# A fused attention, channel-mix and mixture-of-attention kernel, with the order of every engine's instructions listed by hand

## The chip, the cores and the metric

One core of one Trainium2 chip. The number is device time in microseconds (us), the median of several runs of one program. A profiled execution, run apart, gives the trace. Engines: PE is TensorE's matmul, PEld its weight load, DVE is VectorE, ACT ScalarE, POOL GpSimd, SP the engine that issues most of the transfers.

## What is computed

Inputs are q, k, v of shape 4 x 8 x 576 x 64 (batch, heads, positions, width) and the weights of two further layers. The reference, cut to what matters:

```python
# 1: attention; heads 0-3 look back 32 positions, heads 4-7 at every 4th of the last 128
attn = softmax(where(mask, q @ k.T / 8, -1e9)) @ v          # -> x: 4 x 576 x 512
# 2: channel mix
x_prev = x shifted down by one position
xk, xr = mu_k * x + (1 - mu_k) * x_prev, mu_r * x + (1 - mu_r) * x_prev
k = maximum(xk @ w_k, 0)                                    # 512 -> 1024
x = sigmoid(xr @ w_r) * ((k * k) @ w_v)                     # 1024 -> 512
# 3: four experts, each a causal attention of width 64; two are kept per position
for e in range(4):
    ye = softmax(causal((x @ wq[e]) @ (x @ wk[e]).T / 8)) @ (x @ wv[e]) @ wo[e]
    out += gate(x)[e] * ye
```

## The kernel before

All is done on one core, batch by batch, in three stages that overlap. Large products (line 539) work on pairs of tiles: each operand is split into a high and a low part, and a tile of 128 x 288 results is the sum over 4 or 8 slices of three matmuls (high by high, high by low, low by high), so 12 or 24 matmuls that go into one PSUM bank.

Stage 1, batch 0, lasts some 46 us: `turn_qk` turns q and k (line 248), `attn_weights` makes scores (line 302), exponentials (lines 342, 350) and normalised weights (line 354), `attn_values` turns the weights (line 382), copies them out of PSUM (`pts`, line 383, ACT) and multiplies them with v (line 394); ACT copies each half of 288 positions into `x` (line 409). The bank for these halves ("av") is a single one, so the second half's products wait for that copy. As features of x become ready, `mix_feature` mixes them (lines 513, 514, 516, 517).

Stage 2, `dbatch`, has receptance tiles z (`receptance`, tanh on ACT, line 562), key tiles h (`keys`: relu on ACT, line 568; squaring on ACT, line 570, or DVE, line 575; the high part kh on ACT, lines 571 and 576; the low part kl on DVE, lines 572 and 578), and value tiles v (`values_of`: one DVE pass, line 584, empties the bank). In batch 0 the two halves c = 0, 1 of the 576 positions go in turn, and the weights arrive as raw 64-bit words in slices of one megabyte, which `split_cols` turns into high and low parts by five passes (lines 679, 681, 682, 687, 688) of about 0.7 to 1.2 us on ACT and DVE. The banks of the long products are "mm", three that go round; batch 0 adds others. The attention of batches 1 to 3 runs between the products of the batch before: turned on DVE (lines 271, 276), 36 score matmuls per pair of heads (line 318), nine row minima on DVE (line 337), nine exponentials on ACT (line 342).

Stage 3 makes queries, keys and values of the experts (lines 539, 888), scores (lines 982, 984, two banks "sc" in turn), row minima on DVE (line 988), exponentials on ACT (line 994), turned weights (line 1046, copied at lines 1051 and 1053), values (lines 1092, 1106) and the output products (line 1178).

The code traces instructions in program order. The framework then puts them into each engine's queue, in an order that its own model of the times chooses; each engine takes its queue strictly in turn, and semaphores hold an instruction until what it needs is done. A few places are already tied by hand:

```python
def product(o, wts, xs, kts, wsl):                       # line 532 on
    for kt in kts:
        for w, x in ((wh, xh), (wh, xl), (wl, xh)):
            marks["product"] = nc.tensor.matmul(o, w[:, kt, wsl], x[:, kt, :], start=(n == 0), stop=(n == last)).ins

def keys(dp, b, c, fo, kh, kl, xk, wts):                 # batch 0, fo below 2 or above 5
    p = ps(bank(b), f"h_{b}_{c}_{fo}")[:, :CH]
    product(p, wts["k"], xk, range(KT), slice(128 * fo, 128 * fo + 128))
    r = dp.tile([128, CH], F32, tag="r", name=f"r_{b}_{c}_{fo}", bufs=2)
    nc.scalar.activation(r, p, AF.Relu)
    nc.vector.scalar_tensor_tensor(out=r, in0=r, scalar=0.5, in1=p if b else r, op0=ALU.mult, op1=ALU.mult)
    nc.scalar.copy(kh[:, fo, :], r)
    half.tensor_sub(kl[:, fo, :], r, kh[:, fo, :].bitcast(F32))
```

A few places are already tied by hand (`tc.issue_after`, for instance so that the attention matmuls of the later batches stay behind the last long product traced).

Of the kernel before, what the change touches and what calls it, by code (L numbers as in the profile page):

```python
# [15 lines left out]

NEG = -8.0e9
BIG = 3.0e38


@with_exitstack
def tile_dilated_attention__rwkv_channel_mix__moe_attention(
# [258 lines left out]
    def attn_weights(ap, b, hp, qT, kT):  # L281
# [43 lines left out]
        for t0, t1 in ((0, 5), (5, 9)):  # L325
# [7 lines left out]
            for t in range(t0, t1):  # L333
                k0, mask = win(dil, t)
                c0 = WK * (t - t0)
                if b:
                    nc.vector.tensor_tensor_reduce(  # L337
                        out=pe[:, t, :], in0=sc[:, c0 : c0 + WK], in1=mask, scale=-0.125, scalar=BIG,
                        op0=ALU.add, op1=ALU.min, accum_out=st[:, 0, t : t + 1],
# [286 lines left out]
    def run(gen, n=None):  # L626

        while n is None or n > 0:
            try:
                next(gen)  # L630
            except StopIteration:
                return False
            if n is not None:
                n -= 1
        return True
# [133 lines left out]
    with s2:  # L769
# [190 lines left out]
        def scores(b, e):  # L960
# [8 lines left out]
            for t in ([4, 3, 2, (3, 5), 1, 0, (0, 3)] if (b, e) == (B - 1, E - 1) else [*range(NB), (0, NB)]):  # L969
# [8 lines left out]
                for i, (c0, c1) in enumerate(parts):  # L978
# [10 lines left out]
                        out=pe[:tn, PO[t] + c0 : PO[t] + c1], in0=sc, in1=m, scale=-0.125,  # L989
                        scalar=(BIG if i == 0 else st[:tn, 1, t : t + 1]),  # L990
                        op0=ALU.add, op1=ALU.min, accum_out=least,
# [253 lines left out]
        for g in gens.values():  # L1245
            assert not run(g, 1)


# [1 line left out]
_INS = ['q', 'k', 'v', 'moe_mu_k', 'moe_mu_r', 'moe_w_k', 'moe_w_v', 'moe_w_r',  # L1250
# [27 lines left out]
```

## Time and profile before

| | us |
|---|---|
| three runs | 547.4, 548.07, 548.78 |
| median | 548.07 |
| the profiled execution | 548.24 |
| its span, first to last instruction | 546.5 |
| PE busy in the span | 524.7 (96%) |
| DVE, ACT busy | 348.9 (64%), 331.2 (61%) |

A row of a timeline has the start, the length, the engine, the line and the tiles (out<-in); a bracket tells how long the engine was idle before it and what ended that. Matmuls overlap: each lasts some 300 ns by the trace but the next begins some 131 ns later in a dense stretch, so a busy PE may still issue at less than its best. The granted clock is a share of TensorE's full 2.4 GHz; 0.50 is its lower level, 1.2 GHz.

### The profile page before, as it was taken

What the parts mean: (1) busy time and instruction counts of PE and PEld (TensorE: products, weight loads), DVE (VectorE), ACT (ScalarE), POOL (GpSimd) and SP (SyncE); (2) the same over time, 40 slices, a digit from 0 to 9 for tenths busy, and PEclk for the clock granted to TensorE, in tenths of its full rate; (3) what the DMA queues carried; (4) which work ended last, traced back from release to release, by engine and by line L of the source; (5) the groups of instructions that cost most, each with busy time, mean ns of one, the idle gap of its engine ahead of it and who ended that gap; (6) DMA issues with size and microseconds to landing.
All of it is one profiled execution on the core that took longest, in us unless ns stands there. A gap on an engine that the chain in (4) does not pass through costs nothing.

```text
span 546.5 us, 12497 instructions
## 1 busy us (share of the span) xinstructions
PE 524.7 (96%) x4618; PEld 473.8 (87%) x4622; DVE 348.9 (64%) x1136; ACT 331.2 (61%) x945; POOL 96.8 (18%) x169
## 2 busy tenths in 40 slices
PE   8988987999999999999999999999998999999996
PEld 4667987889999999999999999999976988988763
DVE  4787989695667588276461526448676658665742
ACT  3679978675884484564443525237557757656852
POOL 8400000010342021221032203000213212211300
PEclk9996999899999999999999999999999999999999
DMA  9969276876455663130100420054604425516103
GB/s 164 240 215 280 78 196 145 143 136 141 96 115 137 142 141 73 49 99 34 34 1 1 93 64 1 1 131 116 146 22 110 141 69 122 131 48 168 67 33 96
DMA packets 130172, 57.64 MB, mean 105 GB/s; under 512 B 109928, under 2 KB 117184, under 8 KB 130112
## 3 DMA queue, kind: packets, MB, share of 16 engines
q1 hardware_dynamic: 129392, 55.88, 43.5%
q8 instruction: 36, 0.59, 0.5%
q0 software_dynamic: 416, 0.44, 0.4%
q10 hardware_dynamic: 304, 0.53, 0.3%
q14 instruction: 24, 0.20, 0.1%
HBM read 34.42 MB, written 10.03 MB: 81 GB/s over the span
## 4 chain that ended last, share of the span: by engine, by line
PE 73%; DVE 10%; ACT 6%; DMA 4%; SPq 4%; issue 2%; POOL 1%; DVEq 0%; ACTq 0%; POOLq 0%
PE v L539 18%; PE h L539 11%; PE z L539 5%; PE av L1092 5%; PE pv L888 5%; PE pq L539 4%; PE pk L539 4%; PE po L1178 4%; PE pt L1046 4%; PE av L394 3%; PE sc L982 2%; PE sc L984 2%; DMA rqk<-in_k_dram 2%; SPq L189 2%; PE sc L318 2%
## 5 line engine op out<-in xcount | busy, mean ns | idle before, releaser
L539 PE MATMUL v<-kh,wv_hi 128*128 128x288 f32 x256 | 75.7, 303 | 2.5 <-ACT r L568 2.0
L539 PE MATMUL h<-xh,wk_hi 128*128 128x288 f32 x256 | 76.6, 301 | 1.5 <-ACT r L568 0.9
L539 PE MATMUL h<-xl,wk_hi 128*128 128x288 f32 x256 | 75.6, 296 | 0.8 <-DVE xl L517 0.8
L539 PE MATMUL h<-xh,wk_lo 128*128 128x288 f32 x256 | 75.3, 294 | 0.4 <-DVE wk_lo L688 0.4
L539 PE MATMUL v<-kl,wv_hi 128*128 128x288 f32 x256 | 75.4, 299 | 0.0
L539 PE MATMUL v<-kh,wv_lo 128*128 128x288 f32 x256 | 75.3, 299 | 0.0
L1012 POOL TENSOR_SCALAR first<-pe,st 128x64 f32<-128x64 f32 x70 | 31.7, 495 | 151.8 <-DVE st L1006 53.4
L529 POOL TENSOR_TENSOR xl<-m,xh 128x576 fp32r<-128x576 f32 x24 | 35.2, 1484 | 129.6 <-ACT xh L528 97.1
L994 ACT ACTIVATE pe<-pe,st 128x64 f32<-128x64 f32 (+4 forms) x80 | 44.7, 561 | 19.7 <-DVE st L988 19.4
L514 DVE SCALAR_TENSOR_TENSOR m<-x,mus,m 128x288 f32<-128x288 f32 x64 | 30.4, 511 | 34.7 <-ACT m L513 34.7
L539 PEld LDWEIGHTS v<-kh,wv_hi 128*128 128x128 f32 x256 | 48.3, 190 | 3.6 <-ACT r L568 2.4
L539 PEld LDWEIGHTS h<-xh,wk_hi 128*128 128x128 f32 x256 | 47.9, 187 | 3.2 <-ACT r L568 1.4
L539 PEld LDWEIGHTS h<-xl,wk_hi 128*128 128x128 f32 x256 | 48.1, 188 | 1.1 <-DVE xl L517 1.1
L539 PEld LDWEIGHTS h<-xh,wk_lo 128*128 128x128 f32 x256 | 48.2, 188 | 0.7 <-DVE wk_lo L688 0.7
L539 PEld LDWEIGHTS v<-kh,wv_lo 128*128 128x128 f32 x256 | 48.4, 191 | 0.4
L539 PEld LDWEIGHTS v<-kl,wv_hi 128*128 128x128 f32 x256 | 48.4, 191 | 0.4
L342 ACT ACTIVATE pe<-pe,st 128x96 f32<-128x96 f32 x108 | 39.0, 363 | 13.1 <-DVE st L337 13.1
L568 ACT ACTIVATE r<-h 128x288 f32<-128x288 f32 x64 | 25.6, 406 | 34.1 <-PE h L539 27.6
L988 DVE CUSTOM_DVE_ANT_0 pe<-sc,cmask 128x64 f32<-128x64 f32 (+4 forms) x80 | 33.3, 426 | 17.6 <-PE sc L984 15.0
L578 DVE TENSOR_TENSOR kl<-r,kh 128x288 fp32r<-128x288 f32 x50 | 31.0, 625 | 16.5 <-ACT kh L576 16.2
L539 PE MATMUL z<-xl,wr_hi 128*128 128x288 f32 x128 | 38.5, 301 | 0.1
L539 PE MATMUL z<-xh,wr_hi 128*128 128x288 f32 x128 | 38.2, 304 | 0.0
(201 smaller groups left out, 1419.2 us busy)
## 6 DMA issues: line engine op xcount, KB each, us to landing
kk<-kh SPq DMA_DIRECT2D x32, 144.0 KB, 2.7
kl<-kl SPq DMA_DIRECT2D x32, 144.0 KB, 2.8
raw_in_moe_w_k_dram<-in_moe_w_k_dram SPq DMA_DIRECT2D x4, 1024.0 KB, 6.2
raw_in_moe_w_v_dram<-in_moe_w_v_dram SPq DMA_DIRECT2D x4, 1024.0 KB, 6.2
out_dram<-ob SPq DMA_DIRECT2D x14, 256.0 KB, 2.5
rqk<-in_q_dram SPq DMA_DIRECT2D x48, 72.0 KB, 2.5
rqk<-in_k_dram SPq DMA_DIRECT2D x48, 72.0 KB, 2.9
moved<-turned SPq DMA_DIRECT2D x8, 432.0 KB, 3.0
```

The source lines that it names most:

```text
L342: nc.scalar.activation(pe[:, t, :], pe[:, t, :] if b else sc[:, c0 : c0 + WK], AF.Exp, bias=st[:, 0, t : t + 1], scale=-1.0, accum_out=st[ ...
L514: nc.vector.scalar_tensor_tensor(out=m, in0=x, scalar=mus[:, 0, w, f : f + 1], in1=m, op0=ALU.mult, op1=ALU.add)
L529: nc.gpsimd.tensor_sub(lo[:, f], m[:, f], hi[:, f].bitcast(F32))
L539: marks["product"] = nc.tensor.matmul(o, w[:, kt, wsl], x[:, kt, :], start=(n == 0), stop=(n == last)).ins
L568: nc.scalar.activation(r, p, AF.Relu)
L578: half.tensor_sub(kl[:, fo, :], r, kh[:, fo, :].bitcast(F32))
L888: nc.tensor.matmul(p, x[:, kt, t0 : t0 + tn], w[:, kt, 512:772], start=(n == 0), stop=(n == 3 * KT - 1))
L988: nc.vector.tensor_tensor_reduce(out=pe[:tn, PO[t] + c0 : PO[t] + c1], in0=sc, in1=m, scale=-0.125, scalar=(BIG if i == 0 else st[:tn, 1, ...
L994: nc.scalar.activation(pb, pb, AF.Exp, bias=st[:tn, 0, t : t + 1], scale=-1.0, accum_out=st[:tn, 2, t : t + 1])
L1012: nc.gpsimd.tensor_scalar_mul(first["keys"][:, t, e % 2, :], pe[:, PO[t] : PO[t] + 64], st[:, 3, t : t + 1])
L1046: marks[f"turn {b}{e}"] = nc.tensor.transpose(pt[:kn, c0 : c0 + 128], src, ident).ins
L1092: ins = nc.tensor.matmul(av1[p0 : p0 + 64, q0 - 64 : q1 - 64], vh[kb][:kn], w[:kn, c0 : c0 + q1 - q0], start=(kb == blocks[0]), stop=(kb = ...
```

## The change

A table gives, for ACT ("Activation"), SP, DVE, POOL and PE, the order of issue by numbers: n is the n-th instruction of that engine in program order. `issue_in_order`, called at the end of the kernel function, ties each listed instruction behind the one listed before it on its engine, with an edge that carries no semaphore. Left out of the lists are four of the 40 filler matmuls of stage 1 (line 76), one DVE subtraction (line 836) and the first two POOL instructions.

Numbers that matter: ACT 48, 50, 71 are copies into x (line 409), 49, 67, 70, 72 copies of turned weights (line 383), 66 an exponential (line 350), 68 and 142 weight passes (line 679), 69 and 52 weight casts (line 687), 83 the tanh of a z tile, 56 and 77 casts of mixed features, 154 and 155 relu and cast of the last key tile of half 0, 157, 149-151, 159, 153, 152, 156 exponentials. DVE 140 and 153 are squarings, 136, 141, 142, 154 make kl, 143 and 144 are transposes, 155-156, 145-149 and 157-158 row minima, 138 is a weight pass, 106, 108, 110, 112 mix features. PE 209-212 and 217-222 are an attention half, 261-263, 271-273, 563-565 and 584-586 transposes, 655-678 the first value tile, 717-740 and 770-793 the next two, 533-550 and 616-633 scores of the next batch, 979-990, 991-1002, 1021-1032 and 1033-1044 the first four z tiles of batch 1.

```diff
+ORDER = {
+    "Activation": (
...
+        "61-65 31 47 34 49 48 66 35 67-68 50-51 70 72 69 71 52-53 73-74 54 75 55 76 83 56 77-78 88 92 90 94 79 96 84 "
+        "93 86 82 87 89 95 91 80 106 108 102 104 81 97-98 110 114 103 101 107 105 100 99 109 85 111 115 112 116-119 "
+        "123 120 124 121 125-126 113 122 127-129 133 130 134 131 136 135 137-138 132 139 144 140-141 145-148 154 "
+        "161-162 155 157 149-151 159 153 152 156 142 163 158 143 177 160 164 170-171 173-174 179-180 168 175 172 169 "
...
+    "DVE": (
...
+        "52-53 65 49 66 50 67 51 68 20 54-55 40 21 56 69 57-58 41 73 70 74 71-72 42 75 43 76-80 59 81 60-61 82 62 83 "
...
+        "94 115 105 120 116 121-122 117 123-125 128 127 118 129 126 130-132 134-135 133 140 136 143-144 141-142 153 "
+        "155-156 145-147 154 157-158 148-149 137 165 150 184 151 166 138 159 152 160 177 161 139 167-171 178-180 "
...
+    "PE": (
...
+        "249 260 140-143 239-248 252-256 202 257-259 270 282 214-215 148-153 203-204 216 195-200 205-208 261-263 "
+        "271-272 209-212 217-222 273 283-285 264-269 274-281 286-291 293-294 305-306 329-332 341-345 307-310 333-335 "
...
+        "472-487 497-502 488-496 503-505 509-520 506-508 521-529 551-556 530-532 557-562 572-583 634-645 655-663 "
+        "533-550 664-676 717-722 677-678 723-731 770-775 732 616-633 776-778 563 584-585 564-565 779-781 586 782-787 "
...
+        "979-984 951-954 971-978 991-996 985 1021-1027 986-990 1028-1032 997-1000 1033-1035 1001-1002 1036-1044 "
...
+def issue_in_order(tc):
+
+    traced = [i for i in tc.nc.cur_bb.bb.instructions
+              if i.opcode not in ("RegisterMove", "BassTileRelease", "TileRelease", "TilePoolBoundary")]
+    for engine, runs in ORDER.items():
+        mine = [i for i in traced if str(i.engine) == "EngineType." + engine]
+        behind = None
+        for run in runs.split():
+            first, _, last = run.partition("-")
+            for n in range(int(first), int(last or first) + 1):
+                if behind is not None:
+                    tc.add_manual_dep(mine[n], behind.name,
+                                      mybir.DependencyInfo(mybir.DependencyClass.NoSync, mybir.DependencyReason.DATA),
+                                      reason="order of issue")
+                behind = mine[n]
...
+    issue_in_order(tc)
```

## Rows read from the trace of the kernel before

**Rows 1.** The page: span, busy time by engine, granted clock in 40 slices.

```profile
span 546.5 us, 12497 instructions
...
PE 524.7 (96%) x4618; PEld 473.8 (87%) x4622; DVE 348.9 (64%) x1136; ACT 331.2 (61%) x945; POOL 96.8 (18%) x169
...
PEclk9996999899999999999999999999999999999999
```

**Rows 2.** Busy time by stretch: length, each engine, granted clock, DMA share, GB/s.

```profile
36.00:46.00 10.00, 5.64 (x71) 4.23 (x71) 7.12 (x12) 8.16 (x14) 0.00 (x0) 0.65 1.05 393
66.00:72.00 6.00, 4.66 (x31) 3.96 (x31) 6.00 (x13) 4.27 (x10) 0.00 (x0) 1.00 0.20 61
86.00:96.00 10.00, 7.02 (x105) 6.21 (x105) 9.66 (x32) 8.30 (x28) 0.11 (x1) 1.00 0.61 124
96.00:101.00 5.00, 4.45 (x22) 4.44 (x23) 4.26 (x28) 4.73 (x24) 0.00 (x0) 0.66 0.92 181
101.00:140.00 39.00, 38.94 (x483) 35.73 (x482) 26.64 (x103) 23.26 (x84) 2.68 (x4) 1.00 0.73 135
140.00:400.00 260.00, 258.75 (x2363) 252.39 (x2361) 152.32 (x481) 138.96 (x408) 49.17 (x46) 1.00 0.32 76
280.00:300.00 20.00, 20.00 (x153) 20.00 (x152) 4.63 (x11) 6.62 (x15) 4.67 (x4) 1.00 0.00 1
400.00:420.00 20.00, 17.95 (x120) 13.80 (x118) 15.87 (x62) 14.60 (x43) 6.07 (x15) 1.00 0.37 90
500.00:526.00 26.00, 25.01 (x152) 17.46 (x150) 16.87 (x68) 18.51 (x48) 4.57 (x10) 1.00 0.34 108
```

**Rows 3.** Waits of PE, whole span: total us, times, longest.

```profile
PE av L394 <- ACT x L409: 3.8, 3, 1.8
PE sc L982 <- DVE st L988: 2.0, 6, 0.6
```

**Rows 4.** Timeline of ACT and PE from 36 to 45 us: start, length, instruction.

```profile
36.38 0.52 ACT L350 ACTIVATE pe<-pe 128x384 f32<-128x384 f32 x1
...
36.81 0.65 ACT L409 COPY x<-av 128x288 f32<-128x288 f32 x1
...
40.81 0.68 ACT L409 COPY x<-av 128x288 f32<-128x288 f32 x1 [0.78 <-PE av L394]
...
44.14 0.50 ACT L383 COPY pts<-pt 96x384 f32<-96x384 f32 x1
...
37.51 0.45 PE L394 MATMUL av<-pts,vw 96*64 96x32 f32 x8 [1.24 <-ACT x L409]
```

**Rows 5.** Timeline of ACT, DVE and PE from 86 to 99 us.

```profile
88.63 1.16 ACT L679 ACTIVATE raw_in_moe_w_v_dram<-raw_in_moe_w_v_dram 128x1024 f32<-128x1024 f32 x1 [1.41 <-DMA raw_in_moe_w_v_dram<-in_moe_w_v_dram]
...
91.57 0.39 ACT L568 ACTIVATE r<-h 128x288 f32<-128x288 f32 x1
...
96.41 0.41 ACT L576 CAST kh<-r 128x288 fp32r<-128x288 f32 x1
...
86.98 0.77 DVE L276 STREAM_TRANSPOSE qT<-rqk 128x576 f32<-128x576 f32 x1
...
91.80 1.22 DVE L682 SCALAR_TENSOR_TENSOR raw_in_moe_w_v_dram<-raw_in_moe_w_v_dram 128x1024 uint32<-128x1024 uint32 x1
...
94.86 0.45 DVE L575 SCALAR_TENSOR_TENSOR r<-r 128x288 f32<-128x288 f32 x1
...
98.16 0.46 DVE L578 TENSOR_TENSOR kl<-r,kh 128x288 fp32r<-128x288 f32 x1
...
90.76 0.40 PE L539 MATMUL v<-kh,wv_hi 128*128 128x288 f32 x1 [1.24 <-ACT r L568]
```

**Rows 6.** Hand-off of a bank at 100.6 us, and ACT's tanh as a group.

```profile
100.57 0.30 PE L539 MATMUL v<-kh,wv_lo 128*128 128x288 f32 x1
...
100.91 0.46 DVE L584 SCALAR_TENSOR_TENSOR x<-z,v 128x288 f32<-128x288 f32 x1 [0.74 <-PE v L539]
...
L562 ACT ACTIVATE z<-z x32: 381/411/428, 53.7 to 301.2; 128x288 f32<-128x288 f32 x32
```

More of the change, by code (lines that the diff above doesn't have):

```diff
@@ L18 @@
 BIG = 3.0e38
+ORDER = {
+    "Activation": (
[26 rows of a table added]
+    ),
[6 rows of a table added]
+    ),
+    "DVE": (
[30 rows of a table added]
+    ),
+    "Pool": (
[5 rows of a table added]
+    ),
[66 rows of a table added]
+    ),
+}
+def issue_in_order(tc):
[12 more added lines that the diff above has]
+                behind = mine[n]
 @with_exitstack
```

120 rows, old and new, of the table ORDER are left out of this document.

## The prediction

> **What bounds the kernel now.** I read the page first, for the share of each engine and the slices; then the busy time cut into stretches; then TensorE's waits; then the timelines of the stretches where TensorE is idle. The page [rows 1] shows PE busy for 524.7 of 546.5 us. The order cannot change that work, so what it can win is PE's idle time, 21.8 us with the ends, and the time at half clock. The stretches [rows 2] show where that time lies. From 101 to 400 us PE is idle for 0.06 + 1.25 = 1.3 us in 299: nothing is to be won there, and DVE and ACT have 41% and 47% of the time to spare. The holes lie ahead of it (36 to 46 us: 4.4 us; 66 to 72: 1.3; 86 to 96: 3.0; 96 to 101: 0.55) and behind it (400 to 420: 2.05; 500 to 526: 1.0). In two stretches the granted clock is also down, 0.65 from 36 to 46 and 0.66 from 96 to 101. In the holes of the first 101 us DVE or ACT is nearly full (DVE 9.66 of 10 from 86 to 96), so there PE waits for what those engines do in the wrong turn; the waits name them: 3.8 us for ACT's copy of attention values, 2.0 us in six waits for DVE's row minima of the last stage [rows 3].
>
> **The change, part by part.** It adds and removes no instruction. SP's list is the order in which SP issues now, so no transfer passes another; a transfer moves only with its producer. The sum is made against the profiled execution, 548.24 us, of which the span is 546.5 and 1.74 lies around it; the median of the runs is 548.07, 0.17 lower.
>
> A, 36 to 46 us. The copy of the attention half (ACT 48) stands behind an exponential (66) now, at 36.81, and PE's next half starts at 37.51 [rows 4]. The list puts 48 first: 36.81 - 36.38 = 0.43 earlier. It also gives PE transposes 261-263 and 271-272 ahead of that half and the half in one piece, so its own copy (50), now at 40.81, can run behind one weight pass (68), at about 39.3; and it puts the last transposes' copy (72, now at 44.14) before a weight cast (69). Walked on with the lengths of rows 4, the receptance products begin some 2.0 us earlier. But the list also puts the tanh of tile 83 ahead of the casts 56 and 77, so ACT waits there for twelve products at half clock, which I price at half of the gain. I take 1.0; ends 0 and 2.0.
>
> B, 66 to 72 us. PE idles 1.3 us for operands; DVE is full (6.00 of 6). The list does the mixing of the second half (DVE 106 to 112) before four weight passes, part of which now come first. I take 0.5; ends 0 and 1.3, all the idle time there is.
>
> C, 86 to 101 us, the largest. The first value tile needs the last key tile's kl, which DVE makes at 98.16 [rows 5], though the tile's relu ran at 91.57. Between lie ACT's weight pass at 88.63, which first sat 1.41 us for its transfer with the key work behind it, and on DVE a weight pass (91.80, 1.22 us) and the nine minima of the next attention pair, all ahead of the squaring at 94.86 and the cast at 96.41. In the list ACT 142 (that weight pass) stands behind 155 (the cast) and eight exponentials, and DVE has 140, 136, 143-144, 141-142, 153 in a row. From 86.98, with 0.42 to 0.45 for each and about 0.7 for each of the two transposes [rows 5], the squaring 153 ends near 90.5, the cast 155 near 91.3, and kl (154), behind five minima of about 0.2, near 92.3, six us earlier. PE then has value products to do where it now waits. Counting its list off from there, it has done by 97.5 us 49 value products and both sets of scores, of which 40 are done now by 100.7 and nine more take until 101.9: 4.4 us. I subtract 0.7 for the transposes 563-565 and 584-586, which now come where their weights are only just normalised. I take 3.7; ends 0, and 5.2 (3.0 + 0.55 idle, and 5 us x 0.34 of clock).
>
> D, 101 to 400 us, where the list costs. It opens a tile's bank much sooner after the bank's last tile. Counted in PE's order now and in the list, over the 196 tiles of long products, a bank is opened again with nine or fewer matmuls in between twice now and 35 times in the list, with six or fewer never now and 12 times in the list. A hand-off takes from the last product's start to the end of DVE's pass 100.91 + 0.46 - 100.57 = 0.80 us [rows 6], and with ACT's tanh (0.41) about 0.75. A product takes 20 / 153 = 0.131 us [rows 2], so with six in between PE comes back after 7 x 0.131 = 0.92. It fits, by 0.1 us, if the engine is free. If another pass is under way there, PE waits half of 0.45, 0.22; DVE and ACT are busy 59% and 53% of this stretch, so 0.12 on average over random phases, 35 x 0.12 = 4.3. As many of the 35 have more room than the tightest, I take a third, 1.5 us lost; ends 1.3 won and 4.3 lost.
>
> E, 400 to 526 us. The idle time of the two stretches is 3.0 us [rows 2]. Of 96 score tiles, seven open a bank with three or fewer matmuls in between now, and none in the list, so the long waits for the minima go; but with nine or fewer it is 22 now and 28 in the list. I take 1.8 won; ends 3.0 won and 1.0 lost.
>
> The end, 526 us on, has almost the same order: 0. **Sum:** 1.0 + 0.5 + 3.7 - 1.5 + 1.8 = 5.5 us; 548.24 - 5.5 = 542.7, against the median 542.6.
>
> The clock: from 96 to 101 us it stood at 0.66 after a stretch in which PE was idle for 3.0 of 10 us, and from 101 to 400 it stayed at 1.00 [rows 2]. The Trainium skill (TensorE: Matmul & The Clock Gate, "A second HAM failure mode: psum-queue depth-cycling") says that short idles between groups of matmuls, from cycling through PSUM banks, make the clock fall and rise again; this speaks against the list in D, and the trace has no such fall with spaced banks. The third rival below prices it from rows.
>
> **The rivals.** 1) The gain ahead is given back in the product stretch: hand-offs there cost the full 4.3 instead of 1.5, and A and B give nothing. For it: ACT and DVE stay nearly full until 101 us. 5.5 - 2.8 - 1.5 = 1.2 won: 546.9, no difference.
> 2) Slower. The mechanism is the hand-off of banks: 35 product tiles and 28 score tiles, with some twelve transpose tiles, are 75 places where PE, which takes its list strictly in turn, stands if the emptying pass is not next on its engine, and other ready matmuls stand behind it. The gains without any hand-off loss are 1.0 + 0.5 + 3.7 + 3.0 = 8.2, so it decides from 8.2 / 75 = 0.11 us each. At 0.15 each it is 11.3 - 8.2 = 3.1 lost: 551.2. For it: 0.22 is what one pass ahead costs; against it: a third to a half of DVE's and ACT's time is free.
> 3) The clock falls in the product stretch as at 96 us. One fall as there costs 5 x 0.34 = 1.7 us; three of them take the gain to 0.4: 547.7.
> 4) More is won: A keeps 2.0, B 1.3, C 5.2, E 3.0, D nothing: 11.5, 536.6.
> That the list changes nothing I leave out: of 740 ACT instructions 118 keep their place.
>
> **How the numbers follow.** 0.3%, about what a measurement of this kernel can tell from no change, is 1.6 us. The forecast (2 to 9 us won) has 0.64, rival 1 0.13, rival 2 0.10, rival 3 0.04, rival 4 0.09. Faster: the forecast, rival 4 and a third of rival 1, 0.77; same: the rest of rival 1 and rival 3, 0.12; slower: rival 2 and a bit, 0.11. The range reaches from rival 4 (536.6) to 549.2, which takes in rivals 1 and 3 and leaves rival 2 out; the forecast's own range is 539 to 546.
>
> **What would show it.** C right: the first value tile's last product near 93 us instead of 100.57, no clock below 1.00 around 97 us, and 101 us of the old order reached 4 us earlier. A: products from about 45 us. D: PE's idle time from 97 to 396 us near 3 us and in many waits of 0.1 to 0.3 us for ACT or DVE; 6 us and more is rival 1 or 2, a granted clock under 1.00 there rival 3. E: waits of score products for minima well under 2.0 us. The prediction is wrong if PE's share is no higher than 96% by the page, or if the products of the last stage begin no earlier than now.

## The result, and the profile after

| | before | the list |
|---|---|---|
| median, us | 547.74 (4 runs) | 540.67 (4 runs: 540.25 to 543.95) |
| profiled execution, us | 548.24 | 541.05 |
| span | 546.5 | 539.3 |

The list runs in 0.9882 of the time of before, 95% interval 0.984 to 0.9924: 7.1 us won. A second set of runs of the same kernel, on another chip, gave 0.9899 (0.9877 to 0.9921). The prediction was 542.6, with the range 536.6 to 549.2: the sign, the size and the range hold. Two of its five terms, D and E, do not hold, two, A and B, are not shown, and that D and E nearly cancel is luck, as the next sections show.

The page of the list's kernel, the lines of [rows 1]: the dip of the clock in the eighth slice (96 to 109 us) is gone, that in the fourth stays. PE's share is again 96%, although the span is 7.2 us shorter, because PE's own busy time fell by 4.5 us with the same matmuls in the program (four filler matmuls are missing from the trace of before).

```profile
span 539.3 us, 12491 instructions
...
PE 520.2 (96%) x4622; PEld 471.1 (87%) x4622; DVE 348.4 (65%) x1136; ACT 330.6 (61%) x945; POOL 98.0 (18%) x169
...
PEclk9996999999999999999999999999999999999999
```

Busy time by stretch, the list's kernel, columns as in [rows 2] (length, PE, PEld, DVE, ACT, POOL, clock, DMA share, GB/s):

```profile
36.00:46.00 10.00, 6.88 (x76) 5.78 (x75) 8.47 (x13) 9.64 (x17) 0.00 (x0) 0.64 1.05 394
66.00:72.00 6.00, 6.00 (x46) 5.84 (x45) 6.00 (x10) 5.59 (x10) 0.00 (x0) 1.00 0.50 160
86.00:96.00 10.00, 9.92 (x128) 9.01 (x127) 9.18 (x35) 8.26 (x29) 0.11 (x1) 1.00 0.76 172
96.00:101.00 5.00, 5.00 (x45) 4.75 (x40) 4.30 (x25) 4.68 (x18) 0.00 (x0) 1.00 0.69 120
101.00:250.00 149.00, 145.01 (x1578) 137.87 (x1578) 101.63 (x344) 90.97 (x311) 28.59 (x24) 1.00 0.50 105
250.00:400.00 150.00, 148.86 (x1241) 146.24 (x1239) 77.99 (x253) 73.10 (x191) 24.94 (x29) 1.00 0.26 66
400.00:420.00 20.00, 20.00 (x139) 15.70 (x138) 14.64 (x51) 14.65 (x40) 4.63 (x10) 1.00 0.42 103
500.00:526.00 26.00, 26.00 (x166) 20.00 (x162) 16.03 (x64) 19.80 (x51) 2.63 (x6) 1.00 0.34 108
```

The holes of before from 66 to 72, 86 to 101, 400 to 420 and 500 to 526 us are closed. The product stretch has holes now: PE idles 3.99 + 1.14 = 5.1 us from 101 to 400, where it idled 1.3.

**A budget at places of equal work.** Times of a stretch mislead where the work in it has changed. But the two orders of PE can be laid side by side: at some places of the lists (counted from 0: 245, 564, 600, 2044, 2800) both have done exactly the same matmuls. The table has the end of the last matmul up to each such place, read from the timelines; "list, again" is the profile of the second set.

| PE's place, us | before | list | list, again |
|---|---|---|---|
| 245 (attention of pair 0) | 35.92 | 35.06 | 36.06 |
| 564 (ahead of the first value tiles) | 88.32 | 87.39 | 87.35 |
| 600 (first value products) | 93.42 | 91.26 | 91.23 |
| 2044 (last attention of layer 3) | 266.12 | 263.96 | 265.29 |
| 2800 (start of the last stage) | 365.14 | 363.38 | 364.71 |
| PE's end | 541.52 | 534.70 | 535.99 |

So the list wins 2.2 us up to place 600, nothing from there to 2800 (271.7 us before, 272.1 with the list, 273.5 again), and 5.1 us in the last stage (176.4 against 171.3). The profiles differ by up to 1.2 us in when the first loads are there, so single profiles are good to about one us at the first places; the lengths of later stretches repeat far better (the last stage of the list: 171.3 twice).

Between such places progress can be compared too, if each matmul is counted with its usual pace, that is the median time from its start to the next start for its shape in all the profiles. By this count the list is 0.9 us ahead of before at place 564 (some 87 us), 5.2 us at 101 us and 1.8 us at 364 us; in the second profile it is 1.0, 3.4 and 0.4. So a lead is won around the first value tiles and most of it is lost again in the product stretch.

### The profile page after: what moved, and what is told of

Read it like the earlier page. It is cut to its first block, busy times and chain, and to the rows that moved or that the text cites. A ratio compares the mean times of both kernels' runs of the same rounds, so it can differ in the third digit from the quotient of the medians.

```text
span 539.3 us, 12491 instructions
## 1 busy us (share of the span) xinstructions
PE 520.2 (96%) x4622; PEld 471.1 (87%) x4622; DVE 348.4 (65%) x1136; ACT 330.6 (61%) x945; POOL 98.0 (18%) x169
## 4 chain that ended last, share of the span: by engine, by line
PE 58%; ACT 5%; DVE 4%; DMA 3%; issue 1%; SPq 1%; POOL 1%; ACTq 0%
PE v L701 13%; PE h L701 8%; PE av L1254 5%; PE pk L701 5%; PE po L1340 5%; PE pq L701 5%; PE pv L1050 4%; PE pt L1208 4%; PE sc L1146 3%; PE sc L1144 2%; PE z L701 2%; ACT pe L504 2%; PE av L556 1%; DVE kl L740 1%; ACT m L675 1%
## 5 line engine op out<-in xcount | busy, mean ns | idle before, releaser
L1174 POOL TENSOR_SCALAR first<-pe,st 128x64 f32<-128x64 f32 x70 | 33.2, 517 | 143.0 <-DVE st L1168 104.8
L676 DVE SCALAR_TENSOR_TENSOR m<-x,mus,m 128x288 f32<-128x288 f32 x64 | 31.7, 526 | 29.1 <-ACT m L675 28.8
L701 PE MATMUL z<-xh,wr_lo 128*128 128x288 f32 x128 | 37.9, 301 | 0.0
```

The lines of the kernel that those rows point to most:

```text
L676: nc.vector.scalar_tensor_tensor(out=m, in0=x, scalar=mus[:, 0, w, f : f + 1], in1=m, op0=ALU.mult, op1=ALU.add)
L1174: nc.gpsimd.tensor_scalar_mul(first["keys"][:, t, e % 2, :], pe[:, PO[t] : PO[t] + 64], st[:, 3, t : t + 1])
```

## Experiments

All kernels keep every instruction and tile and change only the lists. One thing follows an order without being listed: the framework picks the PSUM bank of a tile anew for each order. In the program of the list 253 of the 496 PSUM tiles lie in another bank than before. relu_first, weight_first, c_act, d_fixed and d_fixed2 have the banks of the list; the kernels that mix two orders and late_empty do not, so what they show is order and banks together. In the diffs of whole stretches, numbers are places of PE's list; in the others, n is the n-th instruction of the engine in program order. Ratios are to the kernel before on the same chip.

### The list for the front alone, and for both ends

```diff
 front_only:      the list up to about 101 us (PE's place 658), then
-                 the list
+                 what is left, in the order of before
 front_and_last:  the same, but from PE's pv_0_4 on again
+                 the list
```

> The list is kept up to about 101 us (the first 658 places of TensorE and what belongs to them on the other engines); from there every engine goes by the order of the kernel before. Theory 1 (the parts add: what is won ahead of 101 us is kept, and the 3.6 us that go lost between 101 and 365 us go lost by the list's order there): products end 6 to 7 us earlier than before all through, the last product of the first value tile of the last stage (pv_0_4) near 359.5 instead of 366.11, last stage 180.4 us long as before, time near 541.5. Theory 2 (the lead at 101 us is only work taken from later, and melts whatever order follows): the lead is under 3 us at 365 us, time 545 or more. Wait of TensorE over 0.6 us between 101 and 365 us: at most two by theory 1.

> The list up to about 101 us, the order of before from there until TensorE has done pv_0_4 (about 365 us), the list again after it. Theory 1 (the parts add, and the list's middle is the only part that costs): 359.5 + 175.0 (the list's last stage) + 1.7 = 536.2, about 4.5 faster than the whole list. Theory 2 (what the list wins in the last stage hangs on its middle, where it made transposes and passes for it ahead of time): the last stage is 177 us or longer, time 538 or more. Against the run with the front alone the difference is the last stage by itself: 5.4 us by theory 1, 1.8 by the prediction.

Measured: 550.23 us (1.0033, 1.0021 to 1.0046) with the front alone, which is slower than before; 544.69 us (0.9945, 0.9929 to 0.9962) with both ends. Waits of PE from 88 to 125 us, then from 366 us on, in the first, and from 365 us on in the second (total us, times, longest):

```profile
PE pt L516 <- DVE pe L488: 2.1, 2, 1.9
PE v L673 <- DVE x L718: 1.5, 1, 1.5
PE v L673 <- DVE kl L706: 0.9, 1, 0.9
PE sc L452 <- DVE kT L405: 0.9, 1, 0.9
...
PE sc L1116 <- DVE st L1122: 2.1, 6, 0.6
```

```profile
PE pk L680 <- DVE ql L1003: 1.0, 1, 1.0
```

Two things follow. The last stage stands by itself: the list there is worth 550.23 - 544.69 = 5.5 us behind an old middle, and 5.1 us behind its own by the table; all six waits for minima are gone, and the rival that it hangs on the middle falls. The front does not stand by itself, so theory 1 of the first run falls. The two numbers of theory 2 came true (no lead is left at 365 us: place 2800 is reached at 367.32 us, 2.2 us later than before), but not its reason that a lead melts whatever follows, since d_fixed below keeps one; here four waits of 5.4 us stand at the seam. The list's front does the key work first and leaves softmax work for later; the order of before then asks at once for the transposes of scores (first row) that DVE has not normalised yet.

### The old order in the middle, and in the front

```diff
 mid_old:  the list to PE's place 600, then
-          the list
+          the order of before to place 2044, then the list
 ab_old:
-          the list to place 600
+          the order of before to place 600
           the list from there
```

> The list up to TensorE's place 600 (about 91 us), the order of before to place 2044 (about 264 us), then the list. At both places TensorE has done the same matmuls in either order. Theory 1 (the first value tiles' gain is given back by the list's order between 101 and 264 us, so the stretch costs 172.7 us in either order): time as the whole list, 540.5 to 541.5. Rival A (the seam costs as in the run with the front alone, since DVE and ACT stand differently than before's order wants): stretch 175 us or more, time 543 or more. Rival B (before's stretch carries a lead on where the list's wastes it): stretch under 171.5, time under 539.5.

> The order of before up to TensorE's place 600 (about 93 us), then the list. Theory 1 (what the list wins up to there, 2.2 us in the profiled run and 3.5 in others, is kept to the end): time 543 to 544.5. Rival (the value tiles after it wait for the weight transfer and for DVE's full queue, which take the lead away; the gain up to 93 us is worth nothing): 540.5 to 541.5, the stretch from place 600 to 2044 two us shorter than the 172.7 to 174.9 of the list.

Measured: 547.2 us (0.9981, 0.997 to 0.9993) and 544.23 us (0.9925, 0.9911 to 0.9939). The stretch from place 600 to 2044 takes 179.4 us in the first, and 173.8 in the second; place 600 is reached at 93.54 there. So what the list wins ahead of 91 us seems to be kept, as theory 1 of that run has it: undoing it costs 1.6 us against the second set of the list, 3.6 against the first, but on another chip, and the intervals of the ratios overlap. The old middle behind the new front is rival A, and one row of ACT in the first kernel shows where it stood longest:

```profile
93.49 1.12 ACT L828 ACTIVATE raw_in_moe_w_v_dram<-raw_in_moe_w_v_dram 128x1024 f32<-128x1024 f32 x1 [6.24 <-DMA raw_in_moe_w_v_dram<-in_moe_w_v_dram]
```

The weight pass 142 that I had found in ACT's way, with a wait of 1.41 us [rows 5], waits 6.24 us here. Its transfer comes later with the list's front, and the next runs are on that.

### The weight pass, and its transfer

```diff
 c_act, Activation:
- ... 140-141 145-148 154 161-162 155 157 149-151 159 153 152 156 142 163 ...
+ ... 140-142 145-148 154 161-162 155 157 149-151 159 153 152 156 163 ...
 weight_first, SP:
- ... 49-59 48 60-64 ...
+ ... 49-52 48 53-64 ...
```

> The whole list, but ACT's pass over the fourth value weight (142) stands again directly behind the key pass 141, ahead of the key work, as before. The transfer that it needs lands near 92 us in the list. Theory 1 (this one place is what held the first value tiles back before): ACT stands from about 87 us for the transfer, the key cast 155 follows at 93 or later instead of 90.2, kl (154) near 94 instead of 90.63, the first value tile ends at 95 to 97 instead of 92.84, and 2 to 4 us go lost, time 542.5 to 545. Rival (DVE's softmax work sets the end of the stretch, and TensorE catches up): the first value tile is late, but time within 1 us of the whole list.

> The whole list; only on SP the transfer of the fourth value weight (48) goes ahead of seven of the eleven q and k transfers that the list leaves in front of it. In the whole list the pass that frees those transfers' buffer (DVE 118) ran at 78.39 instead of 75.35 us, the transfer was issued at 85.48 instead of 82.44 and the weight pass DVE 137 waited for it at 92.2 (0.4 us there, 1.7 us in the run with the relu moved, where TensorE came to the value tiles 1.5 us earlier). Theory 1 (this transfer, not TensorE, sets when the softmax work behind it on DVE is done, and eats a lead won ahead of it): issue near 81.6, no wait of DVE 137, the 1444 matmuls after place 600 take 172 us or less instead of 172.7 to 174.9, time 539 to 540. Rival (DVE and ACT are full there anyway, or the later q and k transfers cost as much): time as the whole list, 540.5 to 541.5.

Measured: 550.71 us (1.0041, 1.0025 to 1.0058) with 142 in its old place, and 543.9 us (0.9923, 0.9904 to 0.9941) with the transfer ahead. Of the longest waits from 84 to 102 us, first kernel, then second:

```profile
PE v L703 <- ACT r L732: 7.9, 1, 7.9
ACT raw_in_moe_w_v_dram L843 <- DMA raw_in_moe_w_v_dram<-in_moe_w_v_dram: 7.2, 1, 7.2
```

```profile
DVE kT L440 <- DMA rqk<-in_k_dram: 3.1, 1, 3.1
...
PE sc L482 <- DVE kT L440: 2.6, 1, 2.6
```

One place in ACT's queue is worth 10.0 us (550.71 - 540.67), or 8.1 against the second set: place 600 comes at 100.67 instead of 91.26, and nothing of it is caught up. That is theory 1, at more than twice its price, because the price is the transfer's lateness, not the pass. Why the transfer is late stands in a few rows. Before, the DVE pass over the first value weight that SP's queue waits for, the issue of the fourth weight's transfer, and the wait of the queue:

```profile
75.35 1.23 DVE L688 TENSOR_TENSOR wv_lo<-raw_in_moe_w_v_dram,wv_hi 128x1024 fp32r<-128x1024 f32 x1 [0.56 <-ACT wv_hi L687]
...
82.44 0.45 SPq L670 DMA_DIRECT2D raw_in_moe_w_v_dram<-in_moe_w_v_dram  x1
...
SPq L176 <- DVE wv_lo L688: 5.2, 1, 5.2
```

With the list, the same pass and issue, the pass that needs the fourth weight, and the wait of the queue:

```profile
78.39 1.22 DVE L850 TENSOR_TENSOR wv_lo<-raw_in_moe_w_v_dram,wv_hi 128x1024 fp32r<-128x1024 f32 x1
...
85.48 0.46 SPq L832 DMA_DIRECT2D raw_in_moe_w_v_dram<-in_moe_w_v_dram  x1
...
92.23 0.69 DVE L843 TENSOR_SCALAR raw_in_moe_w_v_dram<-raw_in_moe_w_v_dram 128x1024 uint32<-128x1024 uint32 x1 [0.43 <-DMA raw_in_moe_w_v_dram<-in_moe_w_v_dram]
...
SPq L338 <- DVE wv_lo L850: 7.9, 1, 7.9
```

The pass at 75.35 frees the buffer into which the next q and k transfers go (SP's queue waits 5.2 us for it before, and 7.9 us with the list); the fourth weight's transfer stands behind eleven of those on SP. The list does that pass 3.0 us later, so all twelve are issued 3.0 us later. An edit agrees: d_fixed2 below puts this pass (DVE 118) earlier again, and the fourth weight's transfer is issued at 83.11 us instead of 84.64 in d_fixed. Putting the weight's transfer ahead of seven of the eleven only made the k transfer the late one (place 600 comes at 93.28 us, 2.0 later than in the list): the rival of that run.

### One relu, and the place of the passes that empty banks

```diff
 relu_first, Activation:
- ... 394 385 387-388 386 370 372 374 373 371 395 397 396 ...
+ ... 394-395 385 387-388 397 386 370 372 374 373 371 396 ...
 relu_first, DVE:
- ... 427 398-402 418-420 403-404 430 405 432 423 ...
+ ... 427 430 398-402 418-420 432 403-405 423 ...
 late_empty (19 exchanges like these), DVE:
- ... 175 203 164 ...   ... 174 195 185 ...   ... 242 251 229 228 ...
+ ... 175 164 203 ...   ... 174 185 195 ...   ... 229 242 251 228 ...
```

> The whole list, but at 237 us ACT's relu of key tile h_2_0_5 (395) goes ahead of nine exponentials and that of h_2_0_6 (397) behind three of them, and DVE takes their second passes (430, 432) correspondingly earlier. Theory 1 (the 2.0 us wait of v_2_0_0 is the relu's place in ACT's queue): that wait falls under 0.5 us, time near 539.0 (1.5 to 2.0 under the whole list), less if the nine exponentials then come late for their transposes. Rival (DVE's late passes at 234 us, one of which took 1.66 instead of 0.45 us, hold all of it up): the wait stays over 1.2 us, time 540 to 541.

> The whole list, but 19 of the 23 passes between 101 and 364 us that empty a bank which TensorE opens again with nine or fewer matmuls in between trade places with the instruction behind them on their engine. In the whole list the openings of such banks cost 0.8 us together, 0.64 of it at one. Theory 1 (a hand-off takes 0.80 us, and a pass ahead adds its length): opening with six in between 0.1 to 0.3 us late, with seven 0.2, with nine 0 but 0.5 behind a transpose of 1.08 us; together 2 to 4 us more, time 542.5 to 545. Rival (hand-offs have much more room than 0.1 us, so their place is of no weight): under 1 us together, time 540 to 541.5.

Measured: 541.52 us (0.9883, 0.9865 to 0.99), the same as the list, and 554.83 us (1.0126, 1.0105 to 1.0147). In the first the wait of 2.0 us at v_2_0_0 is gone, and two others stand behind it, for the next bank and for the key tile's low part; I had put 432 behind a normalisation that waits for the exponentials. So theory 1 has the wait right and the time wrong. PE's waits there, from 236 to 246 us:

```profile
PE v L703 <- DVE kl L742: 1.0, 1, 1.0
PE v L703 <- DVE r L739: 0.8, 1, 0.8
```

The second is the price of the place. Its worst case is a bank that PE opens for a product of z, and the pass on DVE that now stands ahead of the emptying one:

```profile
141.28 0.40 PE L703 MATMUL z<-xh,wr_hi 128*128 128x288 f32 x1 [3.05 <-DVE x L748]
...
140.34 0.52 DVE L678 SCALAR_TENSOR_TENSOR m<-x,mus,m 128x288 f32<-128x288 f32 x1 [2.83 <-ACT m L677]
```

The pass ahead lasts 0.52 us but has itself waited 2.83 us for ACT, and PE has waited for both. Nineteen exchanges of neighbours cost 554.83 - 541.52 = 13.3 us against the first kernel, which ran on the same chip and stands for the list: three times the upper end of what the lengths of the passes would make, and neither theory. The price is not pure: 94 tiles lie in other banks here than in the list. But 10.0 us of it are lost at openings of banks with nine or fewer matmuls in between, where the list loses 0.8.

### Seven exchanges for seven waits

```diff
 d_fixed
- DVE  252 220 ... 310-311 ... 326 332 327 335
+ DVE  220 252 ... 311 310 ... 335 326 332 327
- ACT  230 265-266 268 ... 404 368-369 431 409 407 434
+ ACT  230 266 268 265 ... 404 368-369 409 407 431 434
- ACT  394 385 387-388 386 370 372 374 373 371 395 397 396 398-400
+ ACT  394 385 387 395 397 388 386 396 398 370 372 374 399 373 371 400
- DVE  426 414-417 472 427 398-402 418-420 403-404 430 405 432 423 433 431 429 434-435
+ DVE  426 414-415 427 416-417 398-399 430 400-402 432 472 418-420 433 431 434 403-405 435 423 429
- DVE  442 473 451-452 443 453 444 454 445 455
+ DVE  442 451-452 443-444 453 445 454-455 473
- SP   179-181 160 182
+ SP   160 179-182
```

> The whole list with seven local exchanges between 120 and 262 us, one for each long wait of TensorE there (0.64, 0.47, 0.64, 0.44, 0.68, 2.0 and 0.83 us, 5.7 together): DVE 220 ahead of a transpose that waits for its transfer (252), ACT's relus 266 and 268 ahead of a cast (265), DVE 311 ahead of a transpose that waits for its transfer (310), DVE 335 ahead of a pass over sums (326), the key passes of the tiles h_2_0_4 to h_2_0_7 ahead of exponentials and normalisations on ACT and DVE, the exponentials 409 and 407 and the normalisation of pe_3_3 ahead of mixing passes, and on SP the transfer of turned_2_3 (160) ahead of three q transfers. Theory 1 (what the list loses between 101 and 264 us is these few queue places, not the tight hand-offs, of which it keeps all): the 1444 matmuls after place 600 take 168 to 169.5 us instead of 172.7, time 536.5 to 538. Rival (the engines are full there and a wait moved off one place comes back at the next, as it did when the relu alone was moved): 172 us or more, time 540 to 541.5.

> The whole list unchanged, on the same chip as the version with the seven exchanges: 540.3 to 541.5 us, the stretch after place 600 172.5 to 174.5 us.

> The version with seven exchanges and five more, each again for one wait that its profile shows: ACT's first weight cast (113) and the key passes 125 to 129 ahead of the passes over the second value weight (121, 122), which stood 1.6 us for its transfer, with DVE 118, which frees the q and k transfers' buffer, ahead of 125 (TensorE waited 1.2 us at 76 us, and 1.5 us at 93 us behind the late fourth weight); the tanh of z_0_0_0 (82) ahead of a weight pass (84) (0.8 us at 55); the key passes of h_1_0_0 to h_1_0_2 ahead of a cast and exponentials (0.7 at 153); DVE 336 ahead of a transpose and a normalisation (1.05 at 187); on SP the transfer of turned_3_2 ahead of three v transfers (0.6 at 259). Theory 1 (these are queue places too, each worth its wait): 535 to 537 us, TensorE's place 600 one us earlier and the stretch after it 169 us or less. Rival (up to 101 us ACT and DVE are full, so the weight passes that are put back make something else late, as when the fourth weight's transfer alone was put ahead): place 600 no earlier, 538.5 us or more.

Measured, on one chip: 539.15 us (0.984, 0.9827 to 0.9852) against 542.65 us of the list (0.9899, 0.9877 to 0.9921). The stretch from place 600 to 2044 takes 170.9 instead of 174.1 us. The waits of PE from 88 to 264 us in the list again, then with the exchanges:

```profile
PE av L556 <- DMA rqk<-moved: 1.8, 2, 1.5
PE v L701 <- DVE r L737: 1.8, 1, 1.8
PE v L701 <- DVE x L746: 1.6, 1, 1.6
PE h L701 <- DVE r L737: 0.6, 2, 0.3
```

```profile
PE h L704 <- DVE r L740: 1.4, 2, 0.9
PE v L704 <- DVE x L749: 1.3, 1, 1.3
PE av L559 <- ACT r L733: 0.5, 1, 0.5
```

3.5 us won over the list, and 8.7 over before, by moving a few dozen entries; PE's order and the banks are those of the list, so every hand-off that was tight in the list is as tight. That is theory 1, at about half of its price: of the 5.7 us of waits 3.2 are won (1.8 against the list's first profile, 172.7), and a part comes back at h, as the rival said. The list itself came out 1.1 us longer than expected for this run. Five more exchanges of the same kind in the last run, on another chip, 538.54 us (0.9828, 0.9805 to 0.9851), cannot be told from the seven: the stretch from place 600 to 2044 fell again, to 169.4 us, but place 600 came no earlier (90.66 against 90.37), as the rival had it, and a new wait of 1.6 us opened at h_1_0_6.

## Why the prediction was right, and where it was not

**Ahead of 36 us** I had no term. The stretch from place 100 to 245 takes 17.4 us in every profile with the list's front and 18.2 in the two with the old one: 0.8 won.

The terms against the lead of the list at the places above, in us won (place 564 ends A and B, 101 us ends C, 364 us ends D):

| | predicted | list | list, again |
|---|---|---|---|
| ahead of place 245 | none | 0.9 | -0.1 |
| A and B | 1.5 | 0.1 | 1.1 |
| C | 3.7 | 4.2 | 2.4 |
| D | -1.5 | -3.4 | -3.0 |
| E and the end | 1.8 | 5.1 | 5.1 |
| PE's end | 5.5 | 6.8 | 5.5 |

**A and B** (1.0 and 0.5 predicted, at most 2.0 and 1.3). From place 245 to 564 the list wins 0.1 us in its profile, 1.1 in the second, and 0.1 to 1.7 in all the profiles with its front, so the sum of 1.5 is not shown. (Up to place 600 it is 1.3 us, but place 600 lies behind 91 us, in C's stretch.) The mechanisms can be seen. In A the stretch from place 245 to 292 takes 9.9 us instead of 11.9, the 2.0 that I walked; from there to place 408 it takes 17.0 to 18.5 us instead of 16.1. In the list ACT stands 2.68 us for the tanh that I priced (at 49.83 us), and PE 0.9 us for a later one (first row below); the spread goes with the granted clock from 46 to 64 us, 0.91 in the list's profile and 1.00 in that of relu_first. In B, PE's places 408 to 500, from 63.98 to 78.38 us before, take 12.5 us instead of 14.4, with the hole of [rows 2] from 66 to 72 us closed; but places 500 to 564 take 11.5 instead of 9.9, since PE waits there for relus that stand behind weight passes on ACT, the first of which has waited 1.5 us for its transfer (1.1 us up to 77.2 us and 0.5 up to 79.9, two of the three waits of the second row). So B keeps some 0.4.

```profile
PE z L701 <- ACT z L724: 0.9, 1, 0.9
...
PE h L701 <- ACT r L730: 2.2, 3, 1.1
```

**C** (3.7). The mechanism is right, the first value tile to a few tenths. The minima stand behind the squaring, and the rows of the list's kernel that answer to [rows 5] are ACT's cast and weight pass, and DVE's squaring and kl:

```profile
89.80 0.41 ACT L738 CAST kh<-r 128x288 fp32r<-128x288 f32 x1
...
93.10 1.12 ACT L841 ACTIVATE raw_in_moe_w_v_dram<-raw_in_moe_w_v_dram 128x1024 f32<-128x1024 f32 x1
...
89.08 0.46 DVE L737 SCALAR_TENSOR_TENSOR r<-r 128x288 f32<-128x288 f32 x1 [0.17 <-ACT r L730]
...
90.63 0.45 DVE L740 TENSOR_TENSOR kl<-r,kh 128x288 fp32r<-128x288 f32 x1
```

I had the squaring end at 90.5 (89.5), the cast at 91.3 (90.2) and kl begin at 92.3 (90.63); the first value tile's last product ends at 92.84, where I said 93; and by 97.5 us PE has done 51 value products and both sets of scores, where I counted 49. PE idles 0.1 us from 86 to 101 instead of 3.5, and the clock that stood at 0.66 from 96 to 101 us stays at 1.00. How much C wins is less sure: 4.2 us by the table, 2.4 in the second profile, where PE waits 1.6 us for a pass of DVE behind the late fourth weight. What I had wrong is the sentence "a transfer moves only with its producer": it moves with whatever frees its buffer, too. DVE 118, three us later in the list, took twelve transfers with it. That the list puts 142 behind the key work is what saves it from this; c_act shows 8 to 10 us if it did not.

**D** (1.5 lost, at most 4.3). Here the step fails, twice. First the count: I counted hand-offs of banks with nine or fewer matmuls in between, 35 of them, 12 with six or fewer. These numbers come out when the list's order is laid on the banks of the kernel before. In the banks that the list's own program has, there are 24 and 4. Second the price: I gave each a share of another pass's length. Sixteen such openings of z, h and v tiles lie between 101 and 364 us in the list's kernel. Taken from start to start against the usual pace of their shape, they cost 0.8 us together, of which one has 0.64; the two with six in between cost 0.04. (The shares of DVE's and ACT's time to spare that I gave, 41% and 47%, are those from 140 to 400 us; from 101 on they are 40% and 46%.) The tight hand-off fits because the list puts the emptying pass next on its engine, and late_empty shows what that is worth. PE's idle time nevertheless rose from 1.3 to 5.1 us, in seven waits of 0.4 to 2.0 us from start to start: three at banks with 12 to 24 matmuls in between, two at attention products behind a transfer, one at weights that DVE had not normalised, and one at a tight bank (the 0.64). The first lines of PE's waits from 101 to 400 us in the list:

```profile
PE v L701 <- DVE r L737: 1.8, 1, 1.8
PE av L556 <- DMA rqk<-moved: 0.7, 1, 0.7
PE h L701 <- DVE r L737: 0.6, 2, 0.3
```

The largest, from the list's timelines: a DVE pass ahead of it, the first of a run of exponentials on ACT, the relu, and PE:

```profile
233.76 1.66 DVE L740 TENSOR_TENSOR kl<-r,kh 128x288 fp32r<-128x288 f32 x1
...
237.48 0.37 ACT L504 ACTIVATE pe<-pe,st 128x96 f32<-128x96 f32 x1
...
240.72 0.68 ACT L730 ACTIVATE r<-h 128x288 f32<-128x288 f32 x2
...
241.65 0.40 PE L701 MATMUL v<-kh,wv_hi 128*128 128x288 f32 x1 [1.85 <-DVE r L737]
```

From the second row on stand nine exponentials of 0.36 us; the relu behind them begins to empty the bank that PE opens next, though its tile was done by 238.2. d_fixed moves such places, with the same order on PE and the same banks, and wins 3.2 us back. So the loss came near my worst end with another cause: not how soon a bank is opened again, but what stands in the queue ahead of the pass that empties it, and what that waits for in turn.

**E** (1.8 won, at most 3.0). The last stage wins 5.1 us by the table and 5.5 by the two timed kernels. The count of openings found only a part: of twelve waits of over 0.2 us before (two with the list) four, 1.4 us together, stand at banks with three or fewer matmuls in between; the 22 openings with nine or fewer cost 2.9 us before, and the 28 of the list nothing. So their number was no price. The upper end was not one: I took PE's idle time as all that could be won. A row of before, with the one ahead of it:

```profile
412.13 0.29 PE L984 MATMUL sc<-kl,qs 128*128 128x288 f32 x1
412.84 0.40 PE L982 MATMUL sc<-kk,qs 128*128 128x288 f32 x1 [0.42 <-DVE st L988]
```

The second starts 0.71 us after the first, where 0.14 is the pace of this shape: the wait is 0.57, and the bracket says 0.42, since the end of the first matmul lies 0.29 behind its start. Over the twelve waits the start-to-start excess is 5.2 us, and the idle time in the list of waits 3.0. It is part of why PE's busy time fell by 4.5 us without a matmul less (some 2 us; the rest is not split up here), and so why my test "PE's share above 96%" failed although the forecast held: a share of busy time counts part of each wait as work.

**The rivals.** The first, that the product stretch gives the gain back, happened in D nearly in full size (3.4 us), though not by its hand-offs, and A and B gave little; the time did not follow it because E gave 5.1 us. The second, slower by hand-offs at 0.11 us each, fell: tight openings cost 0.05 each. The third, the clock, fell: it is 1.00 in all stretches from 101 to 526 us. On this the rule of the Trainium skill (TensorE: Matmul & The Clock Gate, "A second HAM failure mode: psum-queue depth-cycling"), weighed there, finds nothing in these traces: the list's tightest stretches show no fall.

The sum came out near the truth by luck: D's missing 1.9 us and E's surplus of 3.3 us work against each other. C and D together win 0.8 us in the list's profile and lose 0.6 in the second, so the sign rests on E, which front_only and front_and_last show by itself (order and banks together).

What stays open: how much of C would be left if its own transfers were in time, since every cut between two orders brought a seam and other banks of its own; which of the last stage's exchanges win its 5.1 us; and what the new banks alone are worth, since no run had the list's order on the old ones.

## What to carry to other kernels

When an order is changed, follow each delayed pass to the buffer that it frees, and that buffer to the queue whose head waits for it: a transfer can move without its producer moving. A pass that empties a bank may be as tight as the hand-off allows, if nothing that itself waits for another engine or a transfer stands ahead of it in its queue; price a place by what the instruction ahead waits for, not by its length. Count hand-offs in the program that the new order gives, since the banks can change with the order. Measure PE's waits from start to start against the pace of the shape, and compare two orders where both have done the same work.

## What was not expected of the hardware

A DVE pass that takes 0.45 us lasts up to 1.72 us while POOL works. In the list's kernel, the group of kl passes (min, median and max in ns) and that of the squarings with one input in PSUM, then the POOL pass beside the long one at 233.76:

```profile
L740 DVE TENSOR_TENSOR kl<-r,kh x50: 409/454/1722, 69.7 to 340.4; 128x288 fp32r<-128x288 f32 x50
...
L737 DVE SCALAR_TENSOR_TENSOR r<-r,h x48: 434/453/456, 150.6 to 339.5; 128x288 f32<-128x288 f32 x48
```

```profile
233.32 1.78 POOL L691 TENSOR_TENSOR xl<-m,xh 128x576 fp32r<-128x576 f32 x1 [1.53 <-ACT xh L690]
```

The long pass ends at 235.42, 0.3 us behind POOL's end at 235.10. Between 100 and 364 us, nine of the 44 kl passes on DVE ran beside a POOL pass and lasted 5.0 us longer together than nine at the usual pace; the squarings, about a dozen of them beside POOL, never took over 0.456. Before the change it is the same (14 passes, 8.5 us), so it is no effect of the list, but the two longest waits of PE in D (at 239.5 and 261.6 us) have a DVE pass ahead of them that was lengthened so, a kl and a normalisation; that it causes them is argued, not shown. The Trainium skill (SBUF — State Buffer, "🔬 SBUF: two separate sides") states that DVE and GpSimd take turns by instruction on a shared pair of ports, among other cases when the DVE operation has two inputs in SBUF; the kl passes have both there, the squarings one in PSUM, so the trace agrees. Two inputs are not the only case in this trace: a pass with one input, over a few sums, lasts up to 1.29 us instead of 0.16, and the four of it that lie beside POOL lost 2.8 us:

```profile
L514 DVE TENSOR_SCALAR st<-st x32: 129/162/1294, 13.3 to 257.0; 128x5 f32<-128x5 f32 x16, 128x4 f32<-128x4 f32 x16
```

No run here took the POOL passes away.
